# Hidden and x tiles at other addresses, state sums beside score matmuls for two groups of units, and halved last stores, in a fused gated-linear-attention and expert-MLP kernel

## The chip, the cores and the metric

One NeuronCore of a Trainium2 chip. The metric is the device time of one execution in microseconds. All runs below are in the fast state (on one core: within 1.5% of the fastest of the same kernel), except that `scan`, a single run, has no state. A ratio is the mean time of one kernel's fast runs over that of the other's of the same rounds, with a 95% interval, so it is not quite the ratio of the medians beside it.

## The reference

```python
# attention: B, H, S, D = 4, 8, 768, 48
for t in range(S):
    state = alpha[:, :, t, :, None] * state + einsum('bhd,bhe->bhde', k[:, :, t], v[:, :, t])
    y[:, :, t] = einsum('bhd,bhde->bhe', q[:, :, t], state)
x = y.transpose(0, 2, 1, 3).reshape(3072, 384)
# four experts, F = 1024
p = domain_probs / (domain_probs.sum(-1, keepdims=True) + 1e-9)
for e in range(4):
    out += p[:, e:e+1] * (np.maximum(x @ w1[e], 0) @ w2[e])
```

## The kernel before

The attention is worked off in 24 units, one per batch and block of 128 time steps; the MLP in groups of units (2, 4, 4, 4, 4, 4, 2). While TensorE multiplies group g through the experts, the units of group g+1 are slipped in between, piece by piece: `attention(u)` is a generator, and a list of "beats" says at which share of the unit's window each of its 17 pieces is issued. There is no scheduler; engine order is the order of issue.

From the second group on, each fp32 product of the MLP is done as three fp32r products. A weight piece, an x tile and a hidden tile (the value behind the ReLU) therefore each have three parts. In the up projection the weights w1 are the stationary operand and x is streamed, 512 columns a time (the matmuls called "one" and "two"); in the down projection the hidden tile is stationary and w2 is streamed, 384 columns a time ("ops").

The pieces of a unit that matter here, with cuts:

```python
# piece 7: "sc", scores of four levels: 64-column tiles, two side by side in the array
for p in range(NP):
    for s in range(2):
        nc.tensor.matmul(out[HALF * s:HALF * (s + 1), 2 * p:2 * p + 2, :],
                         lhsT=KTs[li][:, p, HALF * s:HALF * (s + 1)],
                         rhs=qbs[li][:, p, :, QUAD * s:QUAD * (s + 1)], start=True, stop=True)
# piece 11: "far" (64-column tiles) and sc of two more levels
# piece 15: "yps", the result: 32-column tiles, then a ScalarE copy into x_raw
# piece 16: "sps", the state sum: 128-column stationary operand, only the diagonal halves are used
sps = ps.tile([P, NP, 2, D], F32, name="sps", tag="w")
for p in range(NP):
    nc.tensor.matmul(sps[:, p], lhsT=KB[:, p, :], rhs=rv[:, 2 * p:2 * p + 2, :D], start=True, stop=True)
...
# SBUF, in order of allocation: w2, w1, AT, QT, KT, ..., dec0 to dec6, xT, x_raw, hidden tiles (hT), acc
```

## Time and profile before

| | before |
|---|---|
| device time | 1057.55 us median of 6 runs, 1056.93 to 1061.99 |
| TensorE busy | 98% of the span |
| VectorE, ScalarE busy | 74%, 53% |
| TensorE's waits after 200 us | three, 1.1 us together |

A kernel in this state is read from TensorE's own stream: what kinds of matmul follow each other, and how far apart their starts are. The lines are shown in the prediction.

### The profile page before, as it was taken

To read this page: it belongs to the slowest core of one execution; us is meant where nothing else is said; L and a number is where in the kernel's file an instruction comes from. 1 tells how busy PE (TensorE), PEld (TensorE's weight loads), DVE (VectorE), ACT (ScalarE), POOL (GpSimd) and SP (SyncE) were. 2 spreads that over 40 slices of the span, in tenths; PEclk is the share of its full clock that TensorE was granted. 3 is DMA by queue.
4 is the path that set the end of the run, shared out by engine and by line. 5 is a ranking of instruction groups with operands and counts; after the bars stand their busy time and mean duration, and the time that the engine had idled before them with its cause. 6 is when DMAs were issued, how large, how long until landed. Compare 5 with 4: busy or idle time off the path is not lost.

```text
span 1057.4 us, 21578 instructions
## 1 busy us (share of the span) xinstructions
PE 1039.5 (98%) x8498; PEld 905.3 (86%) x8498; DVE 782.1 (74%) x1620; ACT 565.4 (53%) x1195; POOL 35.5 (3%) x77
## 2 busy tenths in 40 slices
PE   8899999999999999999999999999999999999998
PEld 8777777687877899898898898998989989898988
DVE  5579777678879778678877777986887875656565
ACT  4787777585565654445545536555474453323232
POOL 3000010000001000000000000000000000000000
PEclk9999999999999999999999999999999999999999
DMA  7697699997878956857758659576594454444531
GB/s 119 178 322 223 228 333 347 314 328 246 275 266 296 369 199 219 320 158 292 290 178 331 238 159 362 180 273 254 170 361 191 169 210 179 179 186 173 207 152 46
DMA packets 158837, 251.66 MB, mean 238 GB/s; under 512 B 120112, under 2 KB 135344, under 8 KB 136208
## 3 DMA queue, kind: packets, MB, share of 16 engines
q1 hardware_dynamic: 152688, 208.87, 58.0%
q0 software_dynamic: 5760, 41.29, 9.7%
q8 instruction: 67, 1.10, 0.4%
q14 instruction: 34, 0.28, 0.1%
q10 hardware_dynamic: 288, 0.12, 0.1%
HBM read 207.79 MB, written 42.47 MB: 237 GB/s over the span
## 4 chain that ended last, share of the span: by engine, by line
PE 83%; ACT 4%; DVE 4%; SPq 4%; DMA 3%; issue 2%; POOL 0%; ACTq 0%; DVEq 0%; POOLq 0%
PE ops L650 35%; PE one L557 23%; PE two L557 11%; PE sc L348 5%; PE yps L443 3%; PE tp L270 3%; SPq L214 2%; ACT qb L321 1%; PE one L549 1%; PE sps L478 1%; DMA w<-kept 1%; PE far L403 1%; SPq L215 1%; DMA w<-in_moe_w_dram 1%; DVE w L230 1%
## 5 line engine op out<-in xcount | busy, mean ns | idle before, releaser
L650 PE MATMUL ops<-w,hT 128*128 128x384 f32 x1872 | 347.6, 341 | 0.2 <-DVE hT L603 0.2
L650 PEld LDWEIGHTS ops<-w,hT 128*128 128x128 f32 x1872 | 325.5, 188 | 4.7 <-ACT t L568 0.6
L557 PE MATMUL one<-xT,w 128*128 128x512 f32 x960 | 253.2, 399 | 2.0 <-DMA w<-kept 1.2
L557 PEld LDWEIGHTS one<-xT,w 128*128 128x128 f32 x960 | 176.1, 189 | 40.8 <-DVE QT L328 1.8
L568 ACT ACTIVATE t<-one 128x512 f32<-128x512 f32 (+1 forms) x192 | 107.0, 557 | 177.4 <-PE one L557 171.9
L321 ACT COPY qb<-QT 64x256 f32<-64x256 f32 x336 | 136.6, 407 | 74.3 <-DVE QT L300 40.9
L597 DVE SCALAR_TENSOR_TENSOR hT<-t,hT 128x512 fp32r<-128x512 f32 (+1 forms) x172 | 110.5, 643 | 68.3 <-ACT hT L595 66.0
L570 DVE TENSOR_TENSOR t<-t,two 128x512 f32<-128x512 f32 (+1 forms) x172 | 109.4, 636 | 58.1 <-ACT t L568 29.1
L595 ACT ACTIVATE hT<-t 128x512 fp32r<-128x512 f32 (+1 forms) x172 | 101.8, 592 | 85.9 <-DVE t L570 84.8
L557 PE MATMUL two<-xT,w 128*128 128x512 f32 x480 | 136.5, 393 | 0.0
L557 PEld LDWEIGHTS two<-xT,w 128*128 128x128 f32 x480 | 90.3, 188 | 20.0 <-DVE acc L679 0.2
L603 DVE SCALAR_TENSOR_TENSOR hT<-hT 128x512 fp32r<-128x512 f32 (+1 forms) x172 | 101.1, 636 | 0.0
L650 PE MATMUL ops<-hT 128*128 128x384 f32 x288 | 100.9, 492 | 0.0
L358 DVE COPY_PREDICATED near<-masks,sc 128x256 f32<-128x256 uint8 x144 | 77.0, 535 | 19.2 <-PE sc L348 16.3
L328 DVE TENSOR_TENSOR QT<-QT,dec 128x256 f32<-128x256 f32 x144 | 61.2, 425 | 35.5 <-ACT qb L321 34.8
L348 PEld LDWEIGHTS sc<-qb,KT 128*64 128x64 f32 x2304 | 72.7, 138 | 9.3 <-issue 4.7
L348 PE MATMUL sc<-qb,KT 128*64 128x64 f32 x2304 | 77.2, 223 | 2.6 <-ACT qb L321 2.6
L650 PEld LDWEIGHTS ops<-hT 128*128 128x128 f32 x288 | 52.2, 190 | 29.2 <-DMA hT<-in_moe_w_dram 0.6
L679 DVE SCALAR_TENSOR_TENSOR acc<-ops,p_all,acc 128x384 f32<-128x384 f32 x82 | 49.9, 615 | 29.5 <-PE ops L650 28.4
L341 DVE TENSOR_TENSOR KT<-KT,dec 128x256 f32<-128x256 f32 x144 | 60.3, 419 | 0.0
L340 ACT COPY KT<-KT 128x256 f32<-128x256 f32 x138 | 57.5, 417 | 3.0
L549 PE MATMUL one<-xT,w 128*128 128x256 f32 (+1 forms) x240 | 46.7, 341 | 1.5 <-DMA w<-in_moe_w_dram 0.8
(90 smaller groups left out, 935.2 us busy)
## 6 DMA issues: line engine op xcount, KB each, us to landing
w<-kept SPq DMA_DIRECT2D x144, 1152.0 KB
kept<-w POOLq DMA_DIRECT2D x32, 1152.0 KB, 7.6
hT<-in_moe_w_dram SPq DMA_DIRECT2D x32, 384.0 KB
w<-in_moe_w_dram SPq DMA_DIRECT2D x48, 128.0 KB
ra<-in_alpha_dram SPq DMA_DIRECT2D x23, 192.0 KB
rk<-in_k_dram SPq DMA_DIRECT2D x23, 192.0 KB
rq<-in_q_dram SPq DMA_DIRECT2D x23, 192.0 KB
out_dram<-acc POOLq DMA_DIRECT2D x18, 192.0 KB, 7.0
```

The source lines that it names most:

```text
L321: nc.scalar.copy(out=qb[rows, :, i, :].rearrange("p a (b r) -> p a b r", r=m), in_=qv[rows])
L328: nc.vector.tensor_mul(qv, qv, spread(dv[:, :, :, 0], m))
L341: nc.vector.tensor_mul(new[:, :, :, 0, :], old[:, :, :, 0, :], spread(halved(decs[li])[:, :, :, 1], m))
L348: nc.tensor.matmul(out[HALF * s:HALF * (s + 1), 2 * p:2 * p + 2, :], lhsT=KTs[li][:, p, HALF * s:HALF * (s + 1)], rhs=qbs[li][:, p, :, QUA ...
L358: nc.vector.copy_predicated(near.rearrange("p a (b two r) -> p a b two r", two=2, r=m)[:, :, :, 1, :], mk.unsqueeze(1).broadcast_to([P, H, ...
L557: nc.tensor.matmul(out, lhsT=w[:, part, kc], rhs=x_part(gi, part, kc), start=(part == terms[0] and kc == 0), stop=(part == terms[-1] and k ...
L568: nc.scalar.activation(out=t, in_=one, func=ACT.Copy, scale=FINE)
L570: nc.vector.tensor_add(t, t, two)
L595: nc.scalar.activation(out=top, in_=x, func=ACT.Relu, scale=TRIM)
L597: nc.vector.scalar_tensor_tensor(out=low, in0=x, scalar=0.0, in1=top.bitcast(F32), op0=ALU.max, op1=ALU.subtract)
L603: nc.vector.scalar_tensor_tensor(out=dif, in0=top.bitcast(F32), scalar=1 / 4096.0, in1=low.bitcast(F32), op0=ALU.mult, op1=ALU.subtract)
L650: nc.tensor.matmul(sums[at], lhsT=h, rhs=w, start=(n == begins[at]), stop=(n == ends[at]))
```

## The change

Its intent: TensorE should leave the MLP less often, and come back sooner. The state sum of one unit is cut into 64-column halves and issued beside the far and score matmuls of the next unit; scores of one unit are issued beside the result of the unit before. The beats are new for this, for units 11 to 17; in the built order, pieces of attention stand elsewhere from the 729th to the 2,172nd of the 4,128 MLP matmuls. The hidden tiles and x move in SBUF by a few hundred bytes. The last six stores change queues, and the last two are halved.

```diff
+    PAD = 32
...
+    IN_PAIRS = [*(0.0425 * (j + 1) for j in range(8)), 0.385, 0.43, 0.475, 0.52, 0.6, 0.67, 0.755, 0.84, 1.02]
+    TOGETHER = ((15, 7), (16, 11))
+    in_pairs = range(half + 2 * B + 1, half + 4 * B)
...
-            dec = work.tile([P, NP, P // (2 * m)], F32, name=f"dec{li}", bufs=1)
+            dec = work.tile([P, NP, P // (2 * m)], F32, name=f"dec{li}", bufs=1 + 8 * (li == 6))
...
-                    xraws[gi] = work.tile([P, KC, NT], F32, name="x_raw", bufs=1)
+                    xraws[gi] = work.tile([P, KC * NT + PAD], F32, name="x_raw", bufs=1)[:, :KC * NT]
+                    xraws[gi] = xraws[gi].rearrange("p (c n) -> p c n", n=NT)
...
-            sps = ps.tile([P, NP, 2, D], F32, name="sps", tag="w")
+            apart_ = u + 1 in in_pairs
+            sps = ps.tile([P, NP, 1 if apart_ else 2, D], F32, name="sps", tag="w")
             for p in range(NP):
-                nc.tensor.matmul(sps[:, p], lhsT=KB[:, p, :], rhs=rv[:, 2 * p:2 * p + 2, :D],
-                                 start=True, stop=True)
+                for i in range(2) if apart_ else [slice(0, 2)]:
+                    rows = slice(HD * i, HD * (i + 1)) if apart_ else slice(0, P)
+                    nc.tensor.matmul(
+                        sps[rows, p], lhsT=KB[:, p, rows],
+                        rhs=rv[:, 2 * p + i, :D] if apart_ else rv[:, 2 * p:2 * p + 2, :D],
+                        start=True, stop=True)
...
-            stores.append(lambda: (nc.sync if gi >= LAST - 1 else nc.gpsimd).dma_start(
-                out=out[row:row + P, :], in_=acc))
+            queues = (nc.sync, nc.scalar) if gi == LAST else (nc.gpsimd,)
+            for i, queue in enumerate(queues):
+                rows = slice(P // len(queues) * i, P // len(queues) * (i + 1))
+                stores.append(lambda queue=queue, rows=rows: queue.dma_start(
+                    out=out[row:row + P, :][rows], in_=acc[rows]))
... (the new beats are dealt out so that pieces 7 and 11 of a unit fall on pieces 15 and 16 of the unit ahead; the units of the fourth and fifth groups are spread over a slightly longer time)
```

## The prediction

> **What bounds the kernel now.** I read four views: the page's shares and slices, the stage table, the list of waits of TensorE, and the chain that ended last with its pieces in order of time.
>
> ```profile
> span 1057.4 us, 21578 instructions
> PE 1039.5 (98%) x8498; PEld 905.3 (86%) x8498; DVE 782.1 (74%) x1620; ACT 565.4 (53%) x1195; POOL 35.5 (3%) x77
> PE   8899999999999999999999999999999999999998
> DVE  5579777678879778678877777986887875656565
> PE 83%; ACT 4%; DVE 4%; SPq 4%; DMA 3%; issue 2%; POOL 0%; ACTq 0%; DVEq 0%; POOLq 0%
> ```
>
> TensorE is busy 98% of the span and is 83% of the chain; what isn't TensorE in the chain lies in the first 200 us (slices 1 to 7). The change touches only the attention of the fourth and fifth groups of units, which runs beside the MLP of the third and fourth groups. In the trace a group begins where the up-projection returns to the first weight buffer: at about 343, 510, 677 and 847 us. Those two stages, and the ones after them, are:
>
> ```profile
> 343.00:510.00 167.00, 166.54 (x1408) 149.83 (x1407) 131.29 (x271) 86.17 (x183) 1.63 (x3) 1.00 0.69 250
> 510.00:677.00 167.00, 167.00 (x1412) 150.67 (x1411) 131.32 (x273) 88.70 (x188) 2.15 (x4) 1.00 0.70 251
> 677.00:847.00 170.00, 169.62 (x1546) 151.93 (x1545) 135.68 (x287) 91.89 (x198) 1.92 (x4) 1.00 0.68 243
> 847.00:1057.00 210.00, 206.51 (x1209) 191.69 (x1207) 128.64 (x250) 70.36 (x143) 1.83 (x4) 1.00 0.43 168
> ```
>
> (Columns: stretch, its length, busy us of PE, PEld, DVE, ACT, POOL, clock, DMA share, GB/s.) In the first two stages TensorE has one gap of 0.5 us, at the very start of the first; VectorE is at 79%, ScalarE at 52%, the DMA engines at 69%. After 200 us the whole list of TensorE's waits holds three entries of 0.5 us or less:
>
> ```profile
> PE one L557 <- DVE xT L252: 0.5, 1, 0.5
> PE one L557 <- ACT t L568: 0.4, 1, 0.4
> PE ops L650 <- DVE hT L603: 0.2, 1, 0.2
> ```
>
> So time can be won there only by making TensorE's own stream shorter, and lost only by giving it a wait that it doesn't have now. "Busy" also covers turnarounds between kinds of matmul, so I looked at the chain's pieces (start, length, what) for one unit:
>
> ```profile
> 435.94 1.42 PE yps L443 x52
> 437.36 2.02 PE sc L348 x64
> 439.37 1.58 PE one L557 x6
> 443.70 0.86 PE sps L478 x8
> 444.56 1.42 PE one L557 x6
> 446.66 1.37 PE one L557 x6
> ...
> 456.28 0.59 PE far L403 x8
> 456.87 0.93 PE sc L348 x32
> 457.80 1.61 PE ops L650 x8
> 459.42 0.44 PE tp L270 x4
> ```
>
> The reader should see that six "one" matmuls take 1.37 us undisturbed, 1.42 after the state sum (sps), 1.58 after scores (sc): an excursion into attention costs more than its own matmuls.
>
> **What the Trainium skill says.** The Trainium skill's page "TensorEngine Tiling (Array Packing)", section Tiling Modes, Key Properties: changing the tiling mode, not just the tile, drains TensorE. The trace agrees. From the starts of single matmuls: two 512-column matmuls start 226 to 233 ns apart, but the last one before a 32- or 64-column excursion and the excursion's first 327 ns apart; the 384-column ones 173 to 177, and 261 before far. Leaving costs as much: sc to the next MLP matmul 152 ns against 52 inside, and the MLP's second matmul comes about 100 ns late. From the 32-column yps to the 64-column sc it is 202 against 89.
> The Trainium skill's "TensorE: Matmul & The Clock Gate", section LDWEIGHTS (loading the stationary operand), says that a weight load goes by its columns, P / 1.2 ns, so 107 ns for 128 columns. The eight sps matmuls (128 columns, 96 moving) start 109 to 112 ns apart, the transposes with 128 moving also 111: the load sets the step. Pairs of sc matmuls on the two 64-column halves start 58 ns apart.
> The Trainium skill's "SBUF — State Buffer", section Who interferes with whom: PE and ACT wait for no other engine's port. That speaks against any gain from moving tiles in SBUF. The trace agrees as far as it goes: the same VectorE operation differs by 2% or less between the buffers that it uses.
> The same page, section Door 1: The DMA port swizzle: partitions 0 to 63 reach 8 of 16 ports, all 128 reach 16. No run here shows it yet; it bears on the halved stores.
>
> **The change part by part.**
>
> 1. State sums with scores. In the built program's order the before kernel has 19 excursions "sps" and 23 "far, then two levels of sc" that stand by themselves; the changed one has 12 and 16, and 7 new ones "sps, far, sc" in a row (one of them also has a four-transpose excursion at its end). From the starts, over 13 and 17 cases, with the MLP's own spacing taken off and including the two late matmuls after it: sps alone costs 892 ns (886 to 900), far+sc 1718 (1710 to 1722). Merged and in the same 64-column mode, the state sum adds only its pairs: 4 head pairs x 2 passes = 8 pairs. If the weight load of 64 columns or the step measured for sc sets them, 8 x 58 = 464 ns; if the 48 moving columns instead of 64 do, 8 x 58 x 48/64 = 348. So merged 2066 to 2182 instead of 2610: 428 to 544 saved per unit, 7 units: 3.0 to 3.8 us. I take 3.2.
> 2. Scores with the result: yps+sc in one excursion goes from 13 cases to 15 (in the full form), one sc+yps goes away, lone sc from 7 to 6 and lone yps from 6 to 5. Together costs 3887, apart 1877 + 2212 = 4089; so one more merger is worth 0.2 us. The transposes joined to an excursion once: another 0.1. Sum 0.3. The before kernel had most of this merger already, by luck of its beats.
> 3. Memory. Nine buffers of the last decay tile in place of one (the state update now comes after the next unit has written its own, so more than one is needed) and 128 bytes behind x_raw. In the built program xT and x_raw begin 256 bytes later, the hidden (ReLU) tiles 384 later; the weights stay. Same instructions, same sizes. TensorE's spacing in the before trace has three steady values for 384 columns (173.3, 174.7, 176.7 ns) and two for 512 (229.0, 233.3), but the same loop on the same addresses takes different ones at different times (ops at 866 us 174.7, at 968 us 176.7), so I read it as phase, not address. I count 0.3 us for it and widen the range: if all 1872 and 1440 matmuls of those kinds fell into the best values, (175.1 - 173.3) x 1872 + (230.0 - 229.0) x 1440 = 3.4 + 1.4 us less; into the worst, 3.0 + 4.8 us more.
> 4. Last stores. VectorE's last sum ends at 1054.2, the first packet of its 192 KB store moves 0.85 us later, all packets take 0.67 us, the completion is seen 0.4 us after that, and 1.3 us of fixed ending follow. Halves on two queues can shorten only the 0.67 and a little of the issue; both halves share the 16 DMA engines: 0.1 to 0.3 us. I count 0.2. The four stores before these go from the SP queue to GpSimd's, about 7 us to landing by the page, and they are due near 1037, so they end in time.
>
> Sum: 3.2 + 0.3 + 0.3 + 0.2 = 4.0 us of 1057.7, 0.4%.
>
> **The rivals.**
> A new wait takes it back. The far matmuls need the last level's copies by ScalarE, and in the changed beats stand closer behind them (0.045 of a unit's window instead of 0.085; a window is two units' shares of a 167 us stage of four, 83 us, so 3.8 us instead of 7.1). For this: VectorE at 79% is strictly in order, and four state-update operations now fall next to two score selections and the last key update, about 2.7 us in one place, in the up-projection, where each MLP chunk also needs two VectorE operations of 0.69 us. Against: one chunk of nine MLP matmuls (2.07 us) plus the state sum (0.4) still lies between, the copies take 2 x 0.41, and four PSUM banks hold two chunks. If every unit waited 0.5 us, 7 x 0.5 = 3.5 us would be gone and the time would be about 1057.
> The excursions were hidden anyway. This would hold if something else ended these stages; the empty list of waits from 345 to 677 speaks against it. The time would be unchanged but for the tail, 1057.5.
> Memory position is what matters (the author padded with care): the phase values move as a whole; 1049 to 1062 by the bounds above.
>
> **Range and chances.** The centre is 1057.7 - 4.0 = 1053.7. The excursions are the surest part; the phases and the three runs of before (1057.4 to 1062.0) give about 3 us of scatter, a new wait up to 3.5. Range 1049.5 to 1058. Two per cent would be 21 us either way, five times all that I can find: 0.01 for each, 0.98 within.
>
> **What would show it.** Right: no sps piece of 0.86 us by itself among the seven; pieces sps, far, sc in a row of some 2.0 us; the stretch from the third group's start to the fifth's (343 to 677) shorter by 3 us; TensorE's list of waits between them still empty. Wrong: waits of far or sc for ScalarE or VectorE there; sps pairs at 110 ns instead of 44 to 58; spacings of 384 and 512 columns that keep to one value throughout, or durations of VectorE or ScalarE that shift, which would make memory the cause; the last packets landing later than 1.9 us after VectorE's end.

## The result and the profile after

1052.23 us median of 6 runs (1051.75 to 1056.73) against 1057.55 before; ratio 0.9950, interval 0.9927 to 0.9973. That is 5.3 us, where 4.0 was predicted. The page of the changed kernel, first lines:

```profile
span 1050.8 us, 21723 instructions
PE 1033.8 (98%) x8554; PEld 899.2 (86%) x8554; DVE 778.3 (74%) x1620; ACT 565.7 (54%) x1195; POOL 37.7 (4%) x81
```

VectorE and ScalarE do what they did; TensorE has 56 more matmul records (seven state sums in halves, of eight matmuls more each) and 5.7 us less busy time. Now the chain's pieces around one merged excursion:

```profile
441.57 0.69 PE two L570 x3
442.26 0.60 PE sps L489 x16
442.87 0.45 PE far L410 x8
443.32 0.93 PE sc L355 x32
444.25 1.58 PE one L570 x6
```

Against the lines of before: sps 0.60 instead of 0.86, far 0.45 instead of 0.59 (the entry into 64-column tiles is now paid by sps), and a single late return (1.58) for both. TensorE's waits after 200 us, the whole list; from 345 to 677 us, where the merged excursions are, it is empty, as before:

```profile
PE one L570 <- ACT t L581: 0.4, 1, 0.4
PE ops L663 <- DVE hT L616: 0.2, 1, 0.2
```

One entry of the list before is missing: the wait of 0.5 us for xT at the start of the third group (343 us). With the slow restart behind it, it cost 0.7 us by the starts of the matmuls. It is in all eight traces with the old beats (0.4 to 0.5 us) and in none of the six with the new ones. A score piece of 2.0 us now stands just ahead of that point and would give VectorE the time; that this is the reason is argued, not shown. The prediction had no term for it.

Both kernels run the same 4,128 MLP matmul records in the same order, so the difference can be followed by counting them. At the 800th (297 us) the changed kernel is 0.25 us behind, at the 2,280th (672 us) 4.57 ahead, at the 2,880th 4.78, at the last 6.75. (The span differs by 6.6.) At the 800th and from the 2,280th on, both have the same attention matmuls behind them. So 4.8 us come where the excursions changed: about 3.3 from the excursions, 0.7 from the wait that is gone, the rest from closer MLP matmuls. But 2 us more come after 850 us, where no attention is left and none of TensorE's instructions was changed. That is the stretch to look at. In it the chain has one long piece per expert, 96 down-projection matmuls. Before:

```profile
865.80 16.77 PE ops L650 x96
916.57 16.77 PE ops L650 x96
967.74 16.96 PE ops L650 x96
1019.09 16.96 PE ops L650 x96
```

and after:

```profile
860.85 16.64 PE ops L663 x96
911.45 16.64 PE ops L663 x96
962.05 16.64 PE ops L663 x96
1012.65 16.64 PE ops L663 x96
```

16.96 / 96 is 176.7 ns for one, 16.77 / 96 is 174.7, 16.64 / 96 is 173.3: the three steady values that the prediction took for chance. After the change only the lowest one is left.

### The profile page after: what moved, and what is told of

The parts are those of the page before. It is cut to its first block, busy times and chain, and to the rows that moved or that the text cites. A ratio compares the mean times of both kernels' runs of the same rounds, so it can differ in the third digit from the quotient of the medians.

```text
span 1050.8 us, 21723 instructions
## 1 busy us (share of the span) xinstructions
PE 1033.8 (98%) x8554; PEld 899.2 (86%) x8554; DVE 778.3 (74%) x1620; ACT 565.7 (54%) x1195; POOL 37.7 (4%) x81
## 4 chain that ended last, share of the span: by engine, by line
PE 85%; DVE 5%; ACT 4%; DMA 2%; issue 2%; SPq 1%; POOL 0%; ACTq 0%; DVEq 0%; POOLq 0%
PE ops L663 36%; PE one L570 23%; PE two L570 11%; PE sc L355 6%; PE yps L450 3%; PE tp L277 3%; ACT qb L328 2%; PE one L562 1%; PE sps L489 1%; DMA hT<-in_moe_w_dram 1%; PE far L410 1%; DVE hT L616 1%; DMA w<-in_moe_w_dram 1%; DVE near L365 1%; DVE QT L335 1%
## 5 line engine op out<-in xcount | busy, mean ns | idle before, releaser
L663 PE MATMUL ops<-w,hT 128*128 128x384 f32 x1872 | 342.7, 340 | 0.2 <-DVE hT L616 0.2
L581 ACT ACTIVATE t<-one 128x512 f32<-128x512 f32 (+1 forms) x192 | 106.7, 556 | 175.1 <-PE one L570 169.9
```

The lines of the kernel that those rows point to most:

```text
L581: nc.scalar.activation(out=t, in_=one, func=ACT.Copy, scale=FINE)
L663: nc.tensor.matmul(sums[at], lhsT=h, rhs=w, start=(n == begins[at]), stop=(n == ends[at]))
```

## The experiments

**The same kernel again, the tile moves alone, the rest alone.** Is the new spacing chance or place? The expectations name two theories: by the phase theory a stretch of matmuls falls into one of several spacings by chance; by the memory theory the addresses of the tiles decide. `null` is the kernel before. `mem_only` has only this:

```diff
+            dec = work.tile([P, NP, P // (2 * m)], F32, name=f"dec{li}", bufs=1 + 8 * (li == 6))
...
+                    xraws[gi] = work.tile([P, KC * NT + 32], F32, name="x_raw", bufs=1)[:, :KC * NT]
```

`sched_only` is the changed kernel with dec6's buffers at the far end of SBUF and no padding, so that every other tile lies where it did; `again` is the changed kernel.

> The kernel before, unchanged, as a control. Every theory: ratio 1.000 within about 0.002. It tells how the spacing of the MLP matmuls (173.3, 174.7 or 176.7 ns for 384 columns; 229 or 233 for 512) behaves in another execution of the same program. If the values are chance (phase theory), the stages after 677 us get other values than in the first profile and their total changes by up to 3 us; if addresses or the program set them (memory theory), the same values come back stage by stage.

> The kernel before with the tile moves of the change alone (nine buffers of the last decay tile, 128 bytes behind x_raw); same instruction order. Phase theory: no difference, ratio 1.000 (+-0.002), spacing values of single stretches as mixed as before. Memory theory: about 2 us of the 5.3 us, ratio 0.998, and the mean spacing of the 384-column matmuls after the attention's end (847 us on) falls from about 175.6 to 173.8 ns, as in the changed kernel's profile.

> The changed kernel with all tiles where the kernel before has them (the last decay tile's nine buffers at the far end of the memory); beats, state sums beside scores and halved stores as changed. Phase theory: all of the change's stable gain, 3.4 us from the excursions and 0.2 from the tail, 1053.9 us or 0.9966, and the rest chance. Memory theory: the same 3.6 us here too, but the changed kernel, run beside it, is faster by about 2 us, every time.

> The changed kernel once more, beside the one without the tile moves. Phase theory: the two are equal within 1 us, and both gain 3.6 us on the kernel before. Memory theory: this one is faster by about 2 us, 0.995 against 0.9966, with the mean 384-column spacing in the last stage near 173.8 ns again.

| | median us (runs) | ratio to before | interval |
|---|---|---|---|
| null | 1058.24 (13) | 1.0000 | 0.9992 to 1.0008 |
| mem_only | 1055.39 (10) | 0.9977 | 0.9968 to 0.9986 |
| sched_only | 1053.67 (5) | 0.9961 | 0.9950 to 0.9973 |
| again | 1052.30 (6) | 0.9952 | 0.9939 to 0.9965 |

The control's four long pieces came out like this:

```profile
865.11 16.96 PE ops L650 x96
916.00 16.64 PE ops L650 x96
966.65 16.77 PE ops L650 x96
1017.80 16.96 PE ops L650 x96
```

So which value a stretch gets in the old layout does change from one execution to the next here, as the phase theory says; but the old layout allows three values. (Chance isn't all of it in the old layout either: from the 800th to the 2,280th MLP matmul the two traces of the kernel before agree within 0.02 us.) With the tile moves alone all four pieces take 16.64 us, and the mean spacing of 384-column matmuls is 173.3 to 173.4 ns in each of the four stages from 343 us on, against 174.3 to 175.5 in the two traces of before and 174.2 to 175.0 in `sched_only`. The memory theory is right about the gain: the moves are worth 2.4 us by themselves (1 - 0.9977 of 1058.2; interval 1.5 to 3.4). Between `sched_only` and `again`, 1.4 us by the medians; the intervals of their ratios overlap, so the size on top of the other parts isn't settled better than that.

**Which tile, and against what.** `hid_only` pads x_raw so that the hidden tiles begin 384 bytes later (the sums, acc, which lie behind them and which TensorE doesn't read, move along). `x_only` moves x by 256 bytes as the change does, and the hidden tiles by 2048, which leaves their place within 2 KB unchanged. `all_384` moves everything from the weights on by 384 bytes, so the hidden tiles have the changed kernel's addresses but not its distance to w2. `scan` puts 128 bytes between the four hidden buffers.

```diff
 # hid_only
+xraws[gi] = work.tile([P, KC * NT + 96], F32, name="x_raw", bufs=1)[:, :KC * NT]
 # x_only: dec6 with nine buffers, and
+xraws[gi] = work.tile([P, KC * NT + 448], F32, name="x_raw", bufs=1)[:, :KC * NT]
 # all_384: in the weights' pool, ahead of the first weight tile
+wts.tile([P, 96], F32, name="front", bufs=1)
 # scan: hidden tiles under four names, with a [P, 32] tile between each two
```

> The kernel before with the hidden (ReLU) tiles alone 384 bytes later; xT and x_raw where they were. If the hidden tiles' place sets the spacing of the down projection, 384-column matmuls come every 173.3 ns throughout and the time falls by about 2 us (ratio 0.998), while the 512-column ones keep their mix (about 229.5 to 231). If x is what matters, no change: 1.000 and 175 ns.

> The kernel before with xT and x_raw 256 bytes later, as in the change, and the hidden tiles 2048 bytes later, a shift that leaves their place within 2 KB as it was. Hidden theory: 384-column spacing stays mixed at 174.5 to 175.5, ratio 0.999 or 1.000 (at most 0.5 us from the 512-column matmuls, which would come at 229.0 throughout). X theory: 384-column spacing falls to 173.3 and the time by 2 us.

> The kernel before with every tile from the weights on 384 bytes later: absolute places as new as in the change for the hidden tiles, relative places of weights, x and hidden tiles as before. If absolute addresses (a line or a bank edge) matter, 173.3 ns and 0.998 as with the tile moves alone. If it is the hidden tile's place against the down-projection weights that are read at the same time, the mix stays: 175 ns, 1.000.

> The kernel before with a gap of 128 bytes between the four hidden buffers, so that they begin 0, 128, 256 and 384 bytes later against the weights (within 512 bytes). If the relative place matters, the 384-column spacing differs by the buffer that the loaded weights come from: near 173.3 for the one at 384, above it for the one at 0; the two between tell how wide the good range is. If it doesn't, all four have the same mean.

| | median us (runs) | ratio | interval | 384-column spacing by stage, ns |
|---|---|---|---|---|
| hid_only | 1055.30 (15) | 0.9977 | 0.9970 to 0.9985 | 173.3 |
| x_only | 1057.59 (12) | 1.0002 | 0.9993 to 1.0011 | 174.6 to 175.1 |
| all_384 | 1059.03 (20) | 1.0015 | 1.0008 to 1.0022 | 174.5 to 175.4 |
| scan | 1054.85 (one look) | | | 173.4 to 173.7 |

The long pieces, first with the hidden tiles alone moved, then with everything moved:

```profile
862.57 16.64 PE ops L651 x96
913.16 16.64 PE ops L651 x96
963.76 16.64 PE ops L651 x96
1014.34 16.64 PE ops L651 x96
```

```profile
867.91 16.77 PE ops L651 x96
918.61 16.64 PE ops L651 x96
969.26 16.77 PE ops L651 x96
1020.41 16.96 PE ops L651 x96
```

The whole effect comes with the hidden tiles, the move of x has none, and the new absolute address of the hidden tiles doesn't bring it. What is left is where the stationary operand (hidden) begins against the streamed one (w2): every slice of the two was 64 bytes apart within 512 before, and is 448 apart now. No run moves w2 alone, so that w2 is the partner, and not another tile that the hidden tiles moved against, rests on these two being the operands of the same matmuls. The 512-column matmuls keep near 229 to 230 ns in all of these. In the last stage their value follows the down projection ahead: behind 48 matmuls at 176.6 ns a whole up projection of 72 came at 233.3, five times in four traces, and behind 173.3 or 174.6 ns at 228.9. So part of the gain there is theirs. That the weight load's reads meet the stream's reads inside SBUF would explain it, but this is argued, not shown. `scan` was inconclusive for single distances: buffers alternate every two matmuls, and a short step is followed by a long one (320 to 448: 170.8 ns; 192 to 320: 176.5), so only the overall mean can be read, and it is good too. Why `all_384` is 0.15% slower than before is open; it says that this distance is not the only thing about places that counts.

**State sums beside scores, and their halves.** `no_split` keeps the changed kernel's places but not the halves; `split_all` keeps the places of before and halves all state sums.

```diff
 # no_split, in the changed kernel
-apart_ = u + 1 in in_pairs
+apart_ = False
 # split_all, in the kernel before: the changed kernel's 64-column form for every unit
```

> The changed kernel with the state sums left as 128-column matmuls but standing at the same place, just ahead of far and sc. If the change of tiling mode inside the excursion costs what entering it costs, the merged excursion saves only the MLP's late return, about 0.1 us: about 2500 ns instead of 2187, so 7 x 0.32 = 2.2 us more than the changed kernel, 1054.5 us, 0.997. If standing together alone were the gain, it stays near 2190 and 0.995.

> The kernel before with the state sums in 64-column halves everywhere, places unchanged, so all 19 stand alone between MLP matmuls. From the excursion costs: 8 pairs x 58 plus the fixed cost of a 64-column excursion, about 324 ns, gives 790 instead of 892 ns, 19 x 0.1 = 1.9 us less, ratio 0.998. If the drains cost more than that, 892 or above, 1.000 or slower.

`no_split`: 1054.99 us (7 runs), 0.9978 (0.9965 to 0.9991), 2.7 us above `again` (of other rounds), and by the ratio no better than the tile moves alone (0.9977). `split_all`: 1056.21 us (13 runs), 0.9988 (0.9980 to 0.9996). The excursion of before's width at the new place:

```profile
442.30 0.86 PE sps L489 x8
443.16 0.59 PE far L410 x8
443.75 0.93 PE sc L355 x32
```

Here sps and far take what they took apart. Measured from MLP matmul to MLP matmul with the MLP's own spacing taken off, as in the prediction (medians):

| | excursions | ns |
|---|---|---|
| before: sps, and far+sc elsewhere | 13 and 17 | 892 + 1718 = 2610 |
| no_split: sps+far+sc, sps 128 columns wide | 6 | 2592 |
| split_all: sps in halves, and far+sc elsewhere | 13 and 17 | 799 + 1721 = 2520 |
| after: sps in halves, with far+sc | 6 | 2187 |

Standing together alone gives 18 ns, halving alone 90, both 423. The drain into another tiling mode is paid at each change of mode, not at each leaving of the MLP, so neighbours help only if they share the mode. The starts show it. Whole state sums use the full array, as the MLP does: they start 226 to 235 ns behind the last 512-column matmul, like one more of these, and pay nothing. Halves start 318 to 327 ns behind it. In `no_split` far starts 205 ns behind the whole sums; behind halves it takes 52. `split_all`'s total, 0.09 x 19 = 1.7 us expected from the excursions, measured 1.7 us by the medians and 1.3 by the ratio (0.4 to 2.1), agrees.

**Stores, and a faster version.** `old_stores` is the changed kernel with the last six stores as before. `best` is that with halved state sums in all groups.

```diff
 # old_stores
-queues = (nc.sync, nc.scalar) if gi == LAST else (nc.gpsimd,)
+queues = (nc.sync,) if gi >= LAST - 1 else (nc.gpsimd,)
 # best: the same, and
-apart_ = u + 1 in in_pairs
+apart_ = True
```

> The changed kernel with the last six stores as before, whole and from the SP queue. The traces show 4.22 us from the last matmul to the end with whole stores and 4.42 to 4.51 with halves: so 0.2 to 0.3 us faster than the changed kernel, 0.9950 or a little below, and the last landing 1.9 instead of 2.5 us after VectorE's end. If halves help, it is 0.2 us slower.

> The changed kernel with whole stores as before and the state sums in 64-column halves in all groups, not only beside scores. If a lone 64-column state sum costs about 790 ns, 12 x 0.1 = 1.2 us less than with whole stores alone, so about 1.4 us below the changed kernel: 0.9935 to 0.994. If lone halves cost as much as before, equal to the one with whole stores.

The store's issue at the end of the trace, before and after (two stores in each line; the second number spans both):

```profile
1052.80 1.72 SPq L686 DMA_DIRECT2D out_dram<-QT  x2
```

```profile
1046.05 1.90 SPq L703 DMA_DIRECT2D out_dram<-QT  x2
1046.06 1.89 ACTq L703 DMA_DIRECT2D out_dram<-QT  x2
```

The last issue takes 0.51 us in halves against 0.33 whole, on both queues at once. In the four traces with halves the last landing is 2.44 to 2.50 us after VectorE's last sum and the program ends 4.42 to 4.51 us after the last matmul starts; in the seven with whole stores that I took apart, 1.88 to 1.90 and 4.20 to 4.22. So the halves cost 0.2 to 0.3 us. In total time it doesn't show: `old_stores` is 1052.10 us (6 runs), 0.9952 (0.9937 to 0.9967), the same as `again`. One of its six runs, the profiled one, took 1056.6 us, and its trace shows what this outlier was: a wait at the start of the second group, for a weight transfer, ahead of everything that was changed:

```profile
PE one L570 <- DMA w<-kept: 3.5, 1, 3.5
```

`best` is the fastest kernel measured, 1051.65 us (6 runs, 1050.62 to 1053.24), 0.9942 (0.9931 to 0.9954). Lone halved state sums cost 798 to 819 ns in it, 0.09 less than whole ones, for 12 units 1.1 us; the lead over `old_stores` in the same rounds is 0.45 us by the medians and within the intervals, so it is not settled. Pairing the third group's units too was tried and didn't build: the four query blocks run out. (No run is on record for it.)

## Why the prediction was right, and where it was wrong

The time fell within the range and the mechanism named first was the main one; one step failed outright, another had the wrong sign, and one gain wasn't in the list. The range itself shows little: it reached to 1058, past the unchanged 1057.55. That the total came within 1.3 us is in part luck, since two gains that the prediction didn't count, 2.4 and 0.7 us, stand beside what it did count.

- Bound: right. TensorE's stream set the time of the two stages, and it got no new gap; the one old gap, at their very start, went away (0.7 us, not predicted). The feared wait of far for ScalarE's copies didn't come (list of waits empty, 345 to 677 us). The second rival, that the excursions were hidden anyway, fell with `no_split`.
- Step 1, "merged 2066 to 2182 instead of 2610": measured 2187 (2183 to 2190), 423 ns x 7 = 3.0 us instead of 3.2. The weight load of 64 columns, or the step measured for sc, is the term that holds; the guess that 48 moving columns would be quicker than 64 is not borne out.
- Step 2, 0.3 us: the merged result and scores stay at 3882 to 3889, the joined transposes cost 387 instead of 444: 0.2 + 0.06. Right.
- Step 3, "so I read it as phase, not address. I count 0.3 us": this failed. In one layout a stretch can take any of several values, but the place of the hidden tiles decides which values there are. Measured alone: 2.4 us. The prediction's own sign for it, "spacings of 384 and 512 columns that keep to one value throughout", came true for 384. The third rival, "memory position is what matters", was half right, and the best case worked out there, 3.4 us for the 384-column matmuls, is what the traces show at most. The reasoning slipped in taking "same addresses, different values" as proof against addresses: it shows only that addresses aren't all of it. The place of the two operands within 512 bytes was the same for all 1,872 matmuls, so no comparison inside one trace could have shown it. The page that the prediction leaned on speaks of waits for other engines; here both operands are TensorE's own.
- Step 4, "I count 0.2" saved: the halves cost 0.2 to 0.3. The issue got longer on both queues, which the working had left out.
- Sum: 3.0 + 0.26 + 0.7 + 2.4 - 0.25 = 6.1 us, against 5.3 by the medians (2.9 to 7.7 by the ratio) and 6.6 between the two traces. The schedule and stores alone, 3.7 of it, measured 4.1 us (`sched_only`, 2.9 to 5.3); with the tiles' 2.4 that makes 6.5, and together it was 5.1 in the same rounds (3.7 to 6.5). The intervals allow all of these; whether the parts add up fully isn't settled.

## What to carry to other kernels

When TensorE is the bound and has no gaps, count its excursions between tiling modes, price them from the starts of single matmuls, and merge neighbours only after giving them the same mode. If the same matmuls on the same tiles run at several steady spacings, move the stationary tile against the streamed one by a few hundred bytes and look again; one padded tile tells more than any amount of reading one trace. Price a store's issue too before cutting it in two.

## What the Trainium skill lacked or had wrong

- "SBUF — State Buffer", Who interferes with whom, calls TensorE's two read ports independent and says that PE never waits on anyone. The places of TensorE's own two operands do matter, by whatever cause: 173.3 ns with the hidden tile 448 bytes from w2 within 512, a mix of 173.3, 174.7 and 176.7 at 64; in time 0.9977 with the hidden tile moved and 1.0015 with both moved together. No page has the distance of the two operands.
- "TensorEngine Tiling (Array Packing)", Tiling Modes, Key Properties, names the drain but no size. Here a state sum of eight 58 ns pairs costs 799 ns alone and 2187 - 1721 = 466 beside its kind: some 330 ns for going in, out and back.
- "TensorE: Matmul & The Clock Gate", Back-to-back issue gap, gives N / 2.4 + 2.5 ns when warm, 162.5 for 384 columns and 215.8 for 512. The fp32r stream with a new weight load for each matmul keeps 173.3 and 229.0 at best. The section's own sustained figure for 512 columns, about 131 ns, is far below anything in these fp32r traces, where no two 512-column matmuls start under 225 ns apart.
- "SBUF — State Buffer", "Can I just issue two DMAs to hit both halves?", already says that two concurrent DMAs on the two halves are hardly faster than one of them (+6%). What no page that I used has is the cost for a last store: over two queues each issue takes 0.51 us instead of 0.33, and the last landing comes 2.45 us after VectorE's end instead of 1.89. That 64 partitions reach half the ports (same page, Door 1) fits it; no run here separates the two causes.
